# A written-out order of single instructions, first keys loaded through GpSimd, and three crossed batches instead of four

## The chip, the cores and the metric

The kernel runs on one core of a Trainium2 chip. The metric is the device time of one execution in microseconds, the median of the runs shown. A time of the profile is counted from the first instruction of the span.

## What is computed

A linear attention with random features is followed by a gated long convolution. There are 8 batches, 8 heads, 576 rows and a head size of 64; the model width is 512.

```
q_s, k_s = q * scale, k * scale
phi(x)   = exp(x @ omega.T - |x|^2/2 - max) / sqrt(128)      # 128 features
kv, z    = phi(k_s)^T v,  sum over rows of phi(k_s)
x        = (phi(q_s) kv) / (phi(q_s) z)                      # heads side by side: [8, 576, 512]
x1,x2,x3 = split(x @ w_proj)                                 # three times 512
conv     = irfft(rfft(x2, axis=rows) * rfft(filter, axis=rows))
out      = (x1 * conv * x3) @ w_out                          # [8, 576, 512] in float32
```

## The kernel before, in words

**Attention.** For every batch the first 512 rows are four runs of 128; the other 64 rows of two batches are taken together as the "left" work. The stages of a batch `b`, by the names that the code gives them with `nc.at(stage, b)`, are these:

- "load k", "load q", "load v" (`load_main`) bring the inputs, in float32 in DRAM, into bf16 tiles `kn`, `qn`, `vn`, by loads that GpSimd issues. "load kl", "load ql" and "load vl" (`load_left`) do so for the left rows. The weights `wproj` (three loads) and `wout` and the filter (tiles `yt` and `x13`) come on the same queue.
- "keys" turns `kn` to `kt` (eight transposes on TensorE into the PSUM bank `t`, copied by VectorE), multiplies by the features `om2` (the contraction has 64 rows, so two matmuls can lie beside each other in the array) and takes the exponential on ScalarE to `ek`. "left keys" makes `klt` and `ekl` in the same way.
- "values" finds a maximum over the features on VectorE (`h1`, `mx`), and scales `vn` to `vc` with its reciprocal.
- "turn queries" and "queries" do for `qn`, `qt` and `eqt` what "keys" does for the keys.
- "sums" multiplies `ek` and `vc` to `kv` (40 matmuls of 65 columns).
- "turn out" multiplies `eqt` and `kv`, divides on VectorE (`normalise`: `rden`, then `xb`) and turns the result to `xt`, which has the model width on the partitions.

**The turns.** The dictionary `CROSSED` has, for keys, queries and outputs, the first batch that is turned by a DMA transpose of SP ("cross keys", "cross queries", "cross out") and not by TensorE. For outputs it is 4: batches 4 to 7 are crossed. A crossed output is divided into a tile that shares the buffer of `h1`. One that isn't crossed is divided into `xb`, turned by TensorE in two groups of eight (`turn_back`) into the single buffer of `t`, and copied by ScalarE to `xt`.

**The gated convolution.** It is a transform by matmuls: "fold" and "rest" (sums of thirds of the rows, then a product with the middle third of `wproj`), "forward" (matmuls with tables `fwb`, `fwa`, `fwar`, `fwn`, `fwnr`, then complex products on VectorE, for which SP exchanges halves of a tile, `sw`, `xw`), "gates" (the outer thirds of `wproj`), "inverse" and "out". The tables are made on the chip: "residues" on VectorE and ScalarE (tiles `fi`, `fs`, `yt`, `xt`), "sines" on ScalarE, "tables" by transposes and VectorE copies. "filter" transforms the filter once. The matmuls write the three buffers of PSUM bank `h`, the attention writes the two of `a2`, which has two banks each.

**The start.** The first keys, batch 0's, don't come through GpSimd. `first_keys` has SP load them as float32 into a buffer of the tile `ek`, 512 KB at a time, and VectorE and ScalarE convert one half each. `first_constants` is called after it: it has GpSimd make the counters (`fi`, `x2`) and the identity that the transposes need.

**What sets the order.** The kernel does not issue as it is written. `Plan` records every instruction, with what it reads and writes; matmuls in a row into the same tile in the same stage count as one. `order` then finds the dependencies, gives every recorded instruction a due time from `PERIOD`, `STRETCH` and the tables `LEAD`, `SHIFT` and `LEAN` by stage, batch and engine, and `simulate` runs the recorded list through costs of engines, buffers and DMA queues, and at each step takes the instruction that is due first among those that can start soon. `STAY` favours 64-row matmuls while TensorE is in that form. `issue` emits the list, so every engine gets its instructions in that order and waits for each in turn. Tiles of a pool take their buffers in that order too.

All recorded instructions carry one source line in the profile, the line of `record`'s call in `issue`; they are told apart by tiles.

Of the kernel before, what the change touches and what calls it, by code (L numbers as in the profile page):

```python
# [23 lines left out]
CROSSED = {"keys": 5, "queries": 5, "out": 4}  # L24
PERIOD, STRETCH, STAY = 136.732, 16.038, 101.39
LEAD = {
    "cross keys": 0.92, "cross out": 7.64, "cross queries": -0.74, "filter": 4.65, "fold": -48.94,
    "forward": 107.85, "gates": -40.51, "inverse": 17.39, "keys": -0.75, "left keys": -52.95,
    "left out": -1.12, "left queries": -14.15, "load filter": 50.17, "load k": 55.36,
    "load kl": -1.11, "load q": -0.71, "load ql": 8.56, "load v": 0.49, "load vl": 1.73,  # L30
    "load w0": 1.61, "load w1": 5.28, "load w2": 1.64, "out": -42.88, "queries": 96.24,
    "residues": 1.41, "rest": 14.42, "sines": 0.5, "start": -189.65, "sums": -10.66,
    "tables": 0.2, "turn out": -3.18, "turn queries": 16.85, "values": -5.78, "zeros": 9.94,
}

SHIFT = {
    ("fold", 0): 48.94, ("fold", 1): 188.96, ("fold", 2): 50.05, ("fold", 7): 48.3,
    ("forward", 0): -112.16, ("forward", 1): -114.87, ("forward", 2): -107.32,
    ("forward", 6): -108.25, ("gates", 0): 16.24, ("gates", 1): 40.13, ("gates", 2): 50.94,
    ("gates", 6): 38.24, ("left keys", 2): 53.69, ("left keys", 6): 49.69, ("load k", 2): -56.64,  # L40
    ("load q", 0): -1.89, ("load ql", 0): -33.49, ("load v", 0): 2.07, ("load vl", 2): -6.7,
    ("queries", 1): -97.56, ("queries", 2): -131.03, ("queries", 6): -98.12,
    ("queries", 7): -93.75, ("rest", 1): 207.08, ("rest", 7): -14.42, ("turn out", 1): -12.03,
    ("turn out", 2): -153.32, ("turn queries", 1): -15.77, ("turn queries", 2): -16.64,
    ("values", 1): 546.29, ("values", 2): -24.51,
}
LEAN = {
    ("forward", "DVE"): 35.53, ("forward", "PE"): -40.96, ("gates", "DVE"): -10.03,
    ("gates", "PE"): 146.99, ("keys", "ACT"): -14.86, ("left queries", "ACT"): -47.8,
    ("queries", "ACT"): 5.49, ("queries", "PE"): 33.51, ("rest", "ACT"): -8.58,  # L50
    ("rest", "DVE"): -16.93,
}
# [33 lines left out]
class Op:  # L86
    __slots__ = (
        "eng", "calls", "reads", "writes", "due", "n", "busy", "lat", "deps", "users",
        "tiles", "start", "end", "name", "dma", "table", "where", "rows", "base",
    )  # L90

    def __init__(self, eng, due, n, name, where):
        self.eng, self.due, self.n, self.name, self.where = eng, due, n, name, where
        self.calls, self.reads, self.writes = [], [], []
        self.busy = self.lat = 0.0
        self.deps, self.users = {}, []
        self.tiles = set()
        self.dma = self.table = None
        self.rows = 128
# [13 lines left out]
class Plan:  # L113
# [4 lines left out]
    HOP = {"PE": 55.0, "DVE": 37.0, "ACT": 37.0, "POOL": 60.0, "SP": 60.0}  # L118

    def __init__(self, nc, tc):  # L120
        self.nc, self.tc = nc, tc
        self.ops, self.tile_of, self.slots = [], {}, {}
        self.where = "start", 0
        self.tensor = Proxy(self, "PE", nc.tensor)
        self.vector = Proxy(self, "DVE", nc.vector)
        self.scalar = Proxy(self, "ACT", nc.scalar)
        self.gpsimd = Proxy(self, "POOL", nc.gpsimd)
        self.sync = Proxy(self, "SP", nc.sync)
        self.allow_low_precision = nc.allow_low_precision
# [4 lines left out]
    def _new(self, eng, name):  # L134
        stage, b = self.where
        more = LEAD.get(stage, 0.0) + SHIFT.get((stage, b), 0.0) + LEAN.get((stage, eng), 0.0)
        op = Op(eng, more, len(self.ops), name, self.where)
        self.ops.append(op)
        return op

    def tile(self, pool, shape, dtype, name, bufs=1):
        t = pool.tile(shape, dtype, name=name, bufs=bufs)
        key = t.name if hasattr(t, "name") else t[:].tensor.name
        self.slots[pool.name, name] = bufs
        line = self.where[0]
        self.tile_of[key] = ((pool.name, name), "residues" if line == "load filter" else line)
        return t
# [7 lines left out]
    def record(self, eng, real, name, args, kw):  # L155
# [16 lines left out]
        if join:  # L172
            op = last
        else:
            op = self._new(eng, f"{name} {outs[0].tensor.name}")
            op.rows = ins[0].ap[0][1] if eng == "PE" else 128
# [5 lines left out]
        self._cost(op, eng, name, outs, ins)  # L182
        if name == "activation":
            op.table = {AF.Exp: "exp", AF.Sin: "sin"}.get(kw["func"])
        return op

    def opaque(self, eng, call, out, busy):
# [3 lines left out]
        op.busy = op.lat = busy  # L191

    @staticmethod
    def _free(ap):
        n = 1
        for _, c in ap.ap[1:]:
            n *= c
        return n

    def _cost(self, op, eng, name, outs, ins):  # L200
        out = outs[0]
        n = self._free(out)
        if name == "dma_start_transpose":
            op.busy, op.lat = 2000.0, 2200.0
            op.dma = ("HW", self._free(out) * 128 * 2 / 240.0)
            return
        if name == "dma_start":
            a = out if out.space != bass.MemoryType.DRAM else ins[0]
            run = a.ap[-1][1] * SIZE[a.dtype]
            rows = a.ap[0][1] * self._free(a) // a.ap[-1][1]  # L210
            if eng == "POOL":
                op.busy, op.lat = (880.0 if rows > 600 else 720.0), 3300.0
                op.dma = ("SW", rows * max(run, 166) / 198.0)
            elif out.space != bass.MemoryType.DRAM and ins[0].space == bass.MemoryType.DRAM:
                op.busy, op.lat = 580.0, 2300.0
                op.dma = ("HL", rows * run / 330.0)
            else:
                op.busy, op.lat = 580.0, 2000.0
                op.dma = ("HW", rows * run / 180.0 / (1 if out.space == bass.MemoryType.DRAM else 4))
            return  # L220
        half = all(SIZE[a.dtype] == 2 for a in (out, *ins))
        sbuf = all(a.space != bass.MemoryType.PSUM for a in (out, *ins))
        if eng == "PE":
            m = n / (4.8 if ins[0].ap[0][1] == 64 else 2.4) + 2.5
            op.lat = op.busy + n / 2.4 + 166.0
            op.busy += m
            return
        if eng == "DVE":
            if name == "memset":
                busy = n * SIZE[out.dtype] / 4.8 + 5.0  # L230
            elif name == "reciprocal":
                busy = 5.8 * n + 78.0
            elif name == "tensor_tensor":
                busy = n / (1.92 if half and sbuf else 0.96) + 68.0
            elif name == "scalar_tensor_tensor":
                busy = n / 0.96 + 130.0
            elif name in ("tensor_copy", "tensor_scalar", "tensor_scalar_mul"):
                rate = (4 if sbuf else 2) if half else (2 if sbuf else 1)
                if name != "tensor_copy" and not sbuf:
                    rate = 1  # L240
                busy = n / (0.96 * rate) + (68.0 if half else 100.0)
            elif name == "reduce_max":
                busy = self._free(ins[0]) / 0.96 + 60.0
            else:
                busy = n / 0.96 + 68.0
            op.busy, op.lat = busy, busy + 82.0
        elif eng == "ACT":
            busy = n * 0.8333 + (52.0 if not sbuf else 190.0)
            op.busy, op.lat = busy, busy + 107.0
        else:  # L250
            op.busy = op.lat = n / 1.2 + 100.0

    def order(self):
        last = {}
        for op in self.ops:
# [6 lines left out]
            for key, kind in ((op.reads, 0), (op.writes, 1)):  # L262
                for t, r in key:
                    last[t].append((op, kind, r))
                    if t in self.tile_of:
                        op.tiles.add(t)
        for op in self.ops:
            for o in op.deps.values():
                o.users.append(op)
        for op in reversed(self.ops):  # L270
            lat = op.lat + (op.dma[1] if op.dma else 0.0) + 50.0
            last = min((u.base for u in op.users), default=op.where[1] * PERIOD)
            op.base = last - STRETCH * lat / 1000.0
        for op in self.ops:
            op.due += op.base
            if op.eng == "PE":
# [5 lines left out]
    def simulate(self):  # L282
# [19 lines left out]
        for op in ops:  # L302
            if not op.deps:
                ready[op.eng].append(op)
# [1246 lines left out]
```

## Time and profile before

| what | us |
|---|---|
| three runs | 266.75, 267.43, 267.69 |
| median | 267.43 |
| the profiled execution | 266.88 |
| its span, first to last instruction | 264.8 |
| TensorE busy (PE) | 239.7, 91% |
| VectorE busy (DVE) | 213.4, 81% |
| ScalarE busy (ACT) | 195.2, 74% |
| GpSimd busy (POOL) | 61.3, 23% |

The granted TensorE clock is full throughout. The span is shorter than the execution's own time by 2.1 us, which lie around it. PE is TensorE's matmuls and PEld its weight loads, which overlap them. Matmuls are pipelined and their ends are modelled, so a busy PE need not be at its peak. A line of a timeline has the start, the duration, the engine, the operation, the tiles (out<-in), the shape and a count, and in brackets the idle time before it with what ended it.

### The profile page before, as it was taken

To read this page: it belongs to the slowest core of one execution; us is meant where nothing else is said; L and a number is where in the kernel's file an instruction comes from. 1 tells how busy PE (TensorE), PEld (TensorE's weight loads), DVE (VectorE), ACT (ScalarE), POOL (GpSimd) and SP (SyncE) were. 2 spreads that over 40 slices of the span, in tenths; PEclk is the share of its full clock that TensorE was granted. 3 is DMA by queue.
4 is the path that set the end of the run, shared out by engine and by line. 5 is a ranking of instruction groups with operands and counts; after the bars stand their busy time and mean duration, and the time that the engine had idled before them with its cause. 6 is when DMAs were issued, how large, how long until landed. Compare 5 with 4: busy or idle time off the path is not lost. (4 is left out here: it accounts for less than half of the span.)

```text
span 264.8 us, 5724 instructions
## 1 busy us (share of the span) xinstructions
PE 239.7 (91%) x2202; PEld 135.3 (51%) x2234; DVE 213.4 (81%) x475; ACT 195.2 (74%) x307; POOL 61.3 (23%) x86
## 2 busy tenths in 40 slices
PE   0576689999999999989999999999999999999994
PEld 0444445565476547546456454447455554446541
DVE  7999975689959999998499995979989788188470
ACT  6699499759999988986938976997495565753523
POOL 8634474444831610650040000000000000000000
PEclk9999999999999999999999999999999999999999
DMA  7999999999997978899679169524316311430406
GB/s 178 195 198 189 202 204 200 204 168 188 185 156 132 110 114 159 87 157 189 195 92 177 44 141 220 119 108 135 74 35 182 90 42 38 149 71 2 157 1 198
DMA packets 88866, 36.31 MB, mean 137 GB/s; under 512 B 60299, under 2 KB 83336, under 8 KB 88840
## 3 DMA queue, kind: packets, MB, share of 16 engines
q0 software_dynamic: 58560, 16.78, 61.4%
q1 hardware_dynamic: 30136, 19.04, 29.6%
q8 instruction: 17, 0.28, 0.4%
q10 hardware_dynamic: 144, 0.13, 0.1%
q14 instruction: 9, 0.07, 0.1%
HBM read 34.64 MB, written 9.44 MB: 166 GB/s over the span
## 5 line engine op out<-in xcount | busy, mean ns | idle before, releaser
L405 ACT CAST x<-h 128x512 bf16<-128x512 f32 x68 | 39.8, 596 | 31.5 <-PE h L405 28.4
L405 PE MATMUL h<-xt,wproj 128*128 128x512 bf16 x240 | 59.4, 380 | 1.3 <-DVE bt L405 0.4
L405 PEld LDWEIGHTS <-wproj 128*128 128x128 bf16 x384 | 31.2, 98 | 27.6 <-issue 2.7
L405 ACT ACTIVATE eqt<-a 128x1024 bf16<-128x1024 f32 x32 | 32.2, 1065 | 4.6 <-PE a L405 4.6
L405 ACT ACTIVATE osb<-h 128x512 f32<-128x512 f32 (+4 forms) x49 | 28.2, 575 | 7.3 <-PE h L405 5.9
L405 ACT ACTIVATE ek<-a 128x1024 bf16<-128x1024 f32 x32 | 32.1, 1046 | 0.5 <-PE a L405 0.2
L405 PE MATMUL h<-wproj,xf 128*128 128x512 bf16 x120 | 30.5, 379 | 1.7 <-DVE x13l L405 0.7
L405 PE MATMUL h<-wout,yt 128*128 128x512 bf16 x127 | 30.9, 379 | 0.4 <-DVE yt L405 0.3
L405 POOL DMA_DIRECT2D qn<-in_q_dram x26 | 22.9, 893 | 33.5 <-DMA qt<-qn 19.0
L405 DVE TENSOR_TENSOR x<-h,x 128x512 bf16<-128x512 f32 x32 | 21.8, 684 | 6.4 <-PE h L405 5.6
L405 DVE TENSOR_TENSOR bt<-h,osb 128x384 f16<-128x384 f32 x32 | 16.5, 552 | 7.8 <-PE h L405 5.3
L405 PEld LDWEIGHTS <-yt 128*128 128x128 bf16 x128 | 11.9, 98 | 14.8 <-issue 0.9
L405 PEld LDWEIGHTS <-xf 128*128 128x128 bf16 x134 | 12.2, 98 | 13.9 <-issue 1.5
L405 PE MATMUL h<-x,fwb 128*128 128x512 bf16 x68 | 18.3, 379 | 0.4
L405 PE MATMUL h<-gtab,xs 128*128 128x384 bf16 x64 | 15.6, 326 | 0.0
L405 PE MATMUL a<-om,kt 64*128 64x128 bf16 x256 | 11.5, 218 | 2.9 <-DVE kt L405 1.4
L405 PEld LDWEIGHTS <-eqt 128*128 128x128 bf16 x256 | 10.9, 98 | 5.7 <-DVE xb L405 1.3
L405 DVE TENSOR_TENSOR xb<-a,rden 128x512 bf16<-128x512 f32 x20 | 13.3, 684 | 0.4
L405 PE MATMUL a<-kv,eqt 128*128 128x65 bf16 x256 | 12.0, 194 | 1.0 <-DVE xb L405 1.0
L405 PE MATMUL a<-qt,om 64*128 64x512 bf16 x64 | 11.4, 383 | 0.9 <-ACT eqt L405 0.3
L405 PEld LDWEIGHTS <-kt 64*128 64x128 bf16 x256 | 7.5, 94 | 8.8 <-issue 5.5
L405 DVE TENSOR_TENSOR xf<-xt 128x1024 bf16<-128x1024 bf16 (+1 forms) x16 | 8.6, 551 | 4.2 <-ACT xt L405 4.2
(159 smaller groups left out, 471.2 us busy)
## 6 DMA issues: line engine op xcount, KB each, us to landing
out_dram<-osb SPq DMA_DIRECT2D x24, 256.0 KB, 2.3
vn<-in_v_dram POOLq DMA_DIRECT2D x8, 512.0 KB, 9.6
kn<-in_k_dram POOLq DMA_DIRECT2D x7, 512.0 KB, 8.4
qn<-in_q_dram POOLq DMA_DIRECT2D x24, 128.0 KB, 7.4
sw<-sp SPq DMA_DIRECT2D x16, 128.0 KB, 2.3
wproj<-in_moe_w_proj_dram POOLq DMA_DIRECT2D x3, 512.0 KB, 10.1
ek<-in_k_dram SPq DMA_DIRECT2D x2, 512.0 KB
qn<-in_q_dram POOLq DMA_DIRECT2D x2, 512.0 KB, 10.1
```

Source lines behind the costliest of these rows:

```text
L405: getattr(real, name)(*args, **kw)
```

## The change

It has three parts.

1. `CROSSED["out"]` is 5 in place of 4: batch 4's output is turned by TensorE and ScalarE and not by SP's DMA transpose.
2. `first_keys` is gone. Batch 0's keys are loaded by GpSimd in two halves, and converted on the way; the constants are made by a call between the two halves (the recorded position; the list below decides on the order of issue).
3. `simulate`, the costs and the tables of due times are gone. `ORDER` is a list of the numbers of all 1349 recorded instructions in the order in which they are issued, and `order` returns it.

```diff
-CROSSED = {"keys": 5, "queries": 5, "out": 4}
-PERIOD, STRETCH, STAY = 136.732, 16.038, 101.39
-LEAD = {
...
+CROSSED = {"keys": 5, "queries": 5, "out": 5}
+
+ORDER = """
+    0 28 138 55 1 29 30 136 32 2 33 26 35 4 137 27 3 5 37 31 56 11 38 39 10 22 44 7 48 45 8 49 46
+    50 6 40 52 15 23 51 34 24 84 13 139 41 42 20 47 70 43 21 71 36 77 69 85 25 9 53 86 54 73 57 72
...
+    1316 1267 1306 1265 1318 1266 1268 1269 1331 1270 1317 1332 1335 1334 1333 1338 1336 1337 1341
+    1339 1340 1344 1342 1343 1345 1346 1348 1347
+"""
...
-        return self.simulate()
...
+        order = [self.ops[int(n)] for n in ORDER.split()]
+        place = {op.n: i for i, op in enumerate(order)}
+        assert len(place) == len(order) == len(self.ops)
+        for op in order:
+            assert all(place[n] < place[op.n] for n in op.deps), "an instruction before its data"
+        return order
...
-    def first_keys():
-        nc.at("load k", 0)
-        k32 = nc.tile(att, [P, H, NT, D], FP32, name="ek", bufs=2)
-        t_ = nc.tile(nat, [P, H, NT, D], BF16, name="kn", bufs=2)
-        for g in range(2):
-            hs = slice(4 * g, 4 * g + 4)
-            nc.sync.dma_start(
-                out=k32[:, hs].rearrange("p h t d -> p h (t d)"),
-                in_=k[0, hs, 0:SM, :].rearrange("h (p t) d -> p h (t d)", t=NT),
-            )
-        for g in range(2):
-            hs = slice(4 * g, 4 * g + 4)
-            if g == 0:
-                nc.vector.tensor_copy(out=t_[:, hs], in_=k32[:, hs])
-            else:
-                nc.scalar.copy(out=t_[:, hs], in_=k32[:, hs])
-        nat_tiles["k", 0] = t_
-
-    first_keys()
-    first_constants()
+    load_main(0, "k", 2, first_constants)
     load_main(0, "q")
     load_main(0, "v")
     load_left(0, "k")
```

On each engine the two orders are alike in the large: the stages follow each other in much the same sequence. In the small nearly every engine's list differs. GpSimd's loads are the most mixed. After, they begin: half of batch 0's keys, counters, both left keys, the other half, batch 0's queries, the identity, batch 1's keys, one left value, two left queries, a piece of the filter, batch 0's values. Batch 1's values (`vn`) are the sixth load before and the twenty-fifth after.

## The prediction

> **What bounds the kernel now.** First the busy shares of the page, then its 40 slices (6.6 us each), then the busy time by stretches. In the stretches the columns are busy microseconds and instruction counts of PE, PEld, DVE, ACT and POOL.
>
> ```profile
> PE 239.7 (91%) x2202; PEld 135.3 (51%) x2234; DVE 213.4 (81%) x475; ACT 195.2 (74%) x307; POOL 61.3 (23%) x86
> ...
> PE   0576689999999999989999999999999999999994
> ...
> DVE  7999975689959999998499995979989788188470
> ACT  6699499759999988986938976997495565753523
> ```
>
> ```profile
> 10.00:15.00 5.00, 4.80 (x61) 3.94 (x61) 4.67 (x15) 3.80 (x5) 1.67 (x3) 1.00 1.45 198
> 15.00:20.00 5.00, 3.32 (x44) 1.99 (x41) 4.78 (x15) 5.00 (x7) 1.63 (x2) 1.00 1.46 198
> 30.00:35.00 5.00, 2.99 (x32) 1.60 (x34) 4.90 (x12) 2.99 (x4) 3.86 (x6) 1.00 1.34 199
> 35.00:40.00 5.00, 4.76 (x72) 3.30 (x73) 2.91 (x5) 4.68 (x8) 3.10 (x4) 1.00 1.27 205
> 140.00:150.00 10.00, 9.60 (x90) 5.53 (x90) 9.34 (x21) 8.71 (x15) 0.00 (x0) 1.00 1.03 136
> ```
>
> The kernel has two regimes. Up to about 38 us VectorE sets the pace: from 5 to 35 us it is busy 28.8 of 30 us while TensorE idles 11.7. From 40 us on TensorE sets it: all its stretches from 40 to 260 us sum to 215.45 busy of 220, so it idles 4.55 us there. The rest to 264.8 us is the tail after the last matmul (260.86): one half eviction and a store, in both kernels the same instructions. The clock is granted in full. So the time is: the moment TensorE is filled, plus its work, plus those few idle microseconds.
>
> Two prices are read from TensorE's timeline (start us, us, what; the starts are the clock, since the ends are modelled).
>
> ```profile
> 98.37 1.02 PE L405 MATMUL h<-xt,wproj 128*128 128x512 bf16 x4
> 99.23 0.61 PE L405 MATMUL t<-ident,qn 128*128 128x128 bf16 x8
> 99.68 1.03 PE L405 MATMUL h<-xt,wproj 128*128 128x512 bf16 x3
> ...
> 160.07 1.03 PE L405 MATMUL h<-wout,yt 128*128 128x512 bf16 x4
> 160.94 2.75 PE L405 MATMUL h<-xt,wproj 128*128 128x512 bf16 x12
> 163.62 0.61 PE L405 MATMUL a<-qt,om 64*128 64x512 bf16 x4
> 164.16 1.04 PE L405 MATMUL h<-xt,wproj 128*128 128x512 bf16 x4
> 165.03 1.03 PE L405 MATMUL h<-wout,yt 128*128 128x512 bf16 x4
> ```
>
> A group of eight transposes takes 99.68 - 99.23 = **0.45 us**. Four full matmuls take 0.87 us (160.07 to 160.94), 0.216 each. Twelve, followed by a 64-row block, take 163.62 - 160.94 = 2.68, 0.09 over 12 x 0.216. The block, two pairs side by side, takes 0.54, 0.11 over 2 x 0.216. So going into 64-row work and back costs **0.20 us**.
>
> **What the Trainium skill says.** (1) TensorE: Matmul & The Clock Gate, "Wait — 56ns, not 53.3ns?": warm matmuls start 55.6 ns apart for 128 columns and 215.7 for 512. The trace agrees: 0.45 / 8 = 56 ns and 216 ns. (2) TensorEngine Tiling (Array Packing), "Key Properties": changing the tiling mode drains TensorE; the 0.20 us above fits. (3) DMA: Bandwidth & Descriptors, "SWDGE vs HWDGE vs iDMA": only a GpSimd load casts, and "Issuing engines are not separate DMA queues": all issuers share 16 DMA engines. The trace agrees: behind the 1 MB of SP's uncast keys the first small kl load took 5.45 us to land.
>
> **The change part by part.**
>
> *Batch 4's outputs.* One SP transpose (kernel line "cross out") goes; two groups of eight transposes and two ACT copies come. TensorE: 2 x 0.45 = **+0.90**, on the path, since TensorE idles under 5% there. ACT: 2 x 1.02 (COPY xt<-t, 1022 ns in the groups) = 2.04, beside TensorE: ACT idles 4.6 us from 130 to 140 us. If that cover is gone, they delay the single t bank, up to 1.0 each. DVE: the same four products, into xb instead of h1 (684 and 672 ns): 0. SP: one issue of 1.8 us less; its stores come earlier, nobody waits for them: 0. New are two places where TensorE needs DVE's xb and then, in one PSUM bank, ACT's copy. In the profile such meetings cost 0.2 to 0.9 us (0.69 at 116.62 for a DVE product). I take 0.4 each, **+0.8**, bounds 0 and 2.0.
>
> *64-row blocks.* In the two orders of issue, from the first gate matmul on, I count 35 such blocks before and 33 after: 2 x 0.20 = **-0.4**, bounds -0.4 and 0. Before that point there is one more (12 to 13), under VectorE's pace: 0.
>
> *The first keys.* Gone are two SP loads of 512 KB, a DVE cast of 0.63 us and an ACT cast of 1.05; added are two POOL loads of 256 KB (written), 0.9 us of issue each. ACT's cast filled time in which ACT otherwise waited (below, 2.24 us before the 11.17 row): 0. DVE's 0.63 is a real saving. POOL now issues the first load ahead of the iotas and makes the identity after five loads, at about 6.3 us instead of 1.3. The first TensorE work (4.63, then kl's at 8.07) needs it, but kl lands at about 6, so this is covered.
>
> ```profile
> 8.33 0.60 ACT L405 ACTIVATE gtab<-xt,ph 128x384 bf16<-128x384 f16 x1
> 11.17 0.46 ACT L405 ACTIVATE x<-xt,ph 128x192 bf16<-128x192 f16 x1 [2.24 <-DVE xt L405]
> 11.53 0.44 ACT L405 ACTIVATE gta<-xt,ph 128x192 bf16<-128x192 f16 x1
> 11.98 1.28 ACT L405 ACT_TABLE_LOAD   x1
> 13.28 1.02 ACT L405 ACTIVATE ekl<-a 128x1024 bf16<-128x1024 f32 x1
> ```
>
> *The early order.* These rows show the gate of the start: residues on DVE, last sines, table load, first exponential ekl. After, memsets (vcl 0.50, hqs 0.27, fwar 0.17, small ones) stand ahead of fs, so ACT starts its residues at about 5 instead of 3.78 us and spares its cast. Adding the rows up, its three gtab sines then start near 9.0 and take 1.6, the last two 0.8, the load 1.3: ekl at 12.7 to 13.3. The second half of kt, at 13.49 before, now stands behind h1<-ekl, so after ekl: about 14.5 to 15.8. VectorE waits there for what the cast saved. Five table copies (fwb, fwa, fwar, fwnr: 1.1 us) move from 17 us to behind batch 0's last xb (32.1). So xb comes at -1.7 (no wait) to 0, and vc of batch 1, at 37.95 before, at -0.6 to +0.9. Its user sums starts at 38.69, 0.7 later. I take **0**, bounds -1.7 and +0.9.
>
> *The loads.* From 10 to 58 us POOL's loads land one after another, 2.6 to 2.8 us per 512 KB (qn 10.12, vn 12.81, kn 15.48, vn 18.28, qn 20.93 us). With these steps (0.35 per small load, 0.9 per quarter of qn) the new order lands qn 0 at 10.5, vn 0 at 17, qn 1 at 21.5, wproj 1 at 30.5, vn 1 at **34.4** (18.28 before) and the last wproj at 39.4. They are needed at 14.7, 23.4, 26.3, 42.9, 36.7 and about 47. All are in time: 0. The narrowest is vn 1, with 2.3 us.
>
> *Everything else moved* keeps its size; POOL and SP are re-sorted too, and later POOL waits are behind loads with over 3 us to spare. TensorE's 4.55 us of idle time from 40 to 260 could halve (-2.3) or grow as much; I take 0.
>
> **Sum:** +0.90 + 0.8 - 0.4 = **+1.3 us**. On the profiled execution (266.88 us, its span 264.8 plus 2.1 around it) that is 268.2. The median of the three runs is 0.55 above that execution, so 267.43 + 1.3 = **268.7 us**.
>
> **The rivals.**
>
> *Faster: the order itself pays.* Single instructions, not stages, are placed. If this halves TensorE's idle time (-2.3) and the start keeps VectorE's 0.63, the sum is 0.9 - 0.4 - 2.3 - 0.6 = -2.4: **265.0 us**. For it speaks that stalls such as 0.69 us at 116.62 are waits for one DVE product; against it that only 2% is idle. It decides once idle time from 40 to 260 us is under about 3 us.
>
> *Slower still: vn 1 is late.* It moves from POOL's sixth load to its twenty-fifth. Loads 10% slower than my steps use up its 2.3 us; each further microsecond holds vc, sums of batch 1 and all behind them on DVE. With 2 us late: **270.7 us**. Against it: the DMA engines carry the same bytes less 512 KB of fp32 keys.
>
> *No difference.* The transposes fall into waits that TensorE has anyway (0.4 of idle time from 140 to 150 us), and the blocks save 0.4: +0.1 to +0.5, **267.7 us**.
>
> **How the numbers follow.** My sum 0.40, late loads 0.18, no difference 0.17, faster 0.25. About 0.3% (0.8 us) is what a measurement of this kernel tells from no change. My sum's own range, 267.7 to 270, lies mostly beyond it: slower 0.55, same 0.20, faster 0.25. The range reaches from the faster rival (265.0, taken at 265.2) to late loads with the bank's waits at their bound, 272.0.
>
> **What would show it.** TensorE: 16 transposes t<-ident,xb more (96), idle time 40 to 260 us near 5.3. ACT: xt copies six, no CAST kn. ekl near 13 us; vn 1 landing near 34; first sums of batch 1 near 38.7. I am wrong if TensorE's idle time from 40 us falls, if it is filled over 1 us earlier, or if DVE waits for a load before 60 us.

## The result, and the profile after

| | us |
|---|---|
| after, six runs | 263.25, 264.72, 265.35, 266.06, 266.14, 266.32 |
| median after | 265.71 |
| before, beside it | 266.99 |
| ratio | 0.9924, interval 0.9897 to 0.9950 |
| after, measured once more | ratio 0.9897, interval 0.9862 to 0.9932 |
| the profiled execution of after | 266.32, its span 264.5 |

The change makes the kernel 0.8 to 1.0% faster, 2.0 to 2.8 us. I had forecast 1.3 us slower. The profiled execution is the slowest of the six, and only 0.56 us below that of before (266.88), so its trace shows a bad start as well as the gain.

The page of after: busy time of the engines, then the 40 slices.

```profile
PE 243.5 (92%) x2250; PEld 138.2 (52%) x2250; DVE 211.6 (80%) x474; ACT 194.0 (73%) x308; POOL 63.0 (24%) x88
...
PE   0665969999999999999999999999999999999994
...
DVE  6896795689968999999399897599989889279480
ACT  4796579758999997987958967996495654763533
...
PEclk9998699999999999999999999999999999999999
```

The stretches of after, with the columns as before (the number behind POOL's count is the granted clock):

```profile
10.00:15.00 5.00, 4.43 (x54) 3.34 (x54) 4.06 (x11) 4.97 (x7) 2.56 (x4) 1.00 1.56 183
15.00:20.00 5.00, 3.31 (x50) 2.20 (x48) 4.82 (x11) 4.67 (x6) 3.42 (x5) 1.00 1.57 191
20.00:25.00 5.00, 2.68 (x47) 2.07 (x46) 2.82 (x6) 2.63 (x4) 2.82 (x4) 0.90 1.39 201
25.00:30.00 5.00, 4.31 (x58) 3.60 (x55) 3.59 (x8) 3.69 (x5) 3.00 (x4) 0.50 1.45 195
30.00:35.00 5.00, 3.76 (x54) 2.47 (x52) 4.55 (x11) 1.54 (x3) 2.54 (x4) 0.92 1.60 192
35.00:40.00 5.00, 3.83 (x31) 1.73 (x33) 4.92 (x17) 5.00 (x7) 2.94 (x4) 1.00 1.30 202
140.00:150.00 10.00, 10.00 (x104) 6.08 (x100) 9.17 (x21) 8.81 (x15) 3.89 (x5) 1.00 1.61 161
```

Two things are to be seen. From 40 us on TensorE is no longer idle: its stretches from 40 to 260 us sum to 219.3 of 220. In before they sum to 215.45, but this overstates the difference, since before's trace lacks 32 matmuls (more on this under "Everything else moved" below). And from 20 to 35 us something is wrong that before doesn't have: every engine but the queues is short of work, and then the granted clock falls to half. PE's fifth slice is full only because its matmuls take twice as long.

VectorE's timeline names the wait, and the chain of waits names the load:

```profile
19.76 0.68 DVE L232 TENSOR_TENSOR h<-h 128x1024 bf16<-128x1024 bf16 x1
22.59 0.42 DVE L232 TENSOR_TENSOR vcl<-vl,vcl 64x512 bf16<-64x512 bf16 x1 [2.15 <-DMA vl<-in_v_dram]
```

```profile
5.29 7.55 DMA qn<-in_q_dram
13.12 9.44 DMA vl<-in_v_dram
```

The second half of batch 0's left values was issued at 13.12 us, landed at 22.57, and VectorE, which takes its list in order, waited 2.15 us. Behind it in VectorE's list stood the keys of batch 1 (`kt`), for which TensorE waited. TensorE's timeline, a stall and then sums at half speed:

```profile
24.00 1.04 PE L232 MATMUL a<-om,kt 64*128 64x128 bf16 x16 [2.32 <-DVE kt L232]
25.73 0.61 PE L232 MATMUL a<-qt,om 64*128 64x512 bf16 x2 [0.69 <-ACT ek L232]
26.27 0.61 PE L232 MATMUL t<-ident,ql 128*128 128x128 bf16 x4
26.67 0.26 PE L232 MATMUL a<-vcl,ekl 128*128 128x65 bf16 x1
26.74 0.41 PE L232 MATMUL a<-vc,ek 128*128 128x65 bf16 x4
26.96 0.25 PE L232 MATMUL a<-vcl,ekl 128*128 128x65 bf16 x1
```

A head's five sums come every 0.29 us here (26.67 to 26.96). In the second profile of after, where the clock is full at that time, they come every 0.16:

```profile
23.04 0.62 PE L232 MATMUL a<-om,kt 64*128 64x128 bf16 x16 [1.35 <-DVE kt L232]
24.55 0.39 PE L232 MATMUL a<-qt,om 64*128 64x512 bf16 x2 [0.89 <-ACT ek L232]
24.88 0.40 PE L232 MATMUL t<-ident,ql 128*128 128x128 bf16 x4
25.46 0.19 PE L232 MATMUL a<-vcl,ekl 128*128 128x65 bf16 x1 [0.19 <-ACT ek L232]
25.49 0.29 PE L232 MATMUL a<-vc,ek 128*128 128x65 bf16 x4
25.62 0.19 PE L232 MATMUL a<-vcl,ekl 128*128 128x65 bf16 x1
```

### The profile page after: what moved, and what is told of

Same layout as the page of the kernel before. It is cut to its first block, busy times and chain, and to the rows that moved or that the text cites. A ratio compares the mean times of both kernels' runs of the same rounds, so it can differ in the third digit from the quotient of the medians.

```text
span 264.5 us, 5749 instructions
## 1 busy us (share of the span) xinstructions
PE 243.5 (92%) x2250; PEld 138.2 (52%) x2250; DVE 211.6 (80%) x474; ACT 194.0 (73%) x308; POOL 63.0 (24%) x88
## 4 chain that ended last, share of the span: by engine, by line
PE 77%; DMA 7%; DVE 6%; ACT 5%; issue 2%; POOL 1%; SPq 1%; DVEq 0%; POOLq 0%
PE h L232 60%; PE a L232 13%; PE t L232 4%; DMA vl<-in_v_dram 4%; DMA qn<-in_q_dram 3%; ACT ek L232 2%; SPq L232 1%; DVE x L232 1%; DMA xw<-xr 1%; DVE xb L232 1%; DVE kt L232 1%; ACT qt L232 1%; POOL kn L232 1%; ACT x L232 1%; DVE yt L232 1%
## 5 line engine op out<-in xcount | busy, mean ns | idle before, releaser
L232 PE MATMUL h<-xt,wproj 128*128 128x512 bf16 x256 | 62.8, 380 | 0.0
L232 ACT ACTIVATE osb<-h 128x512 f32<-128x512 f32 (+4 forms) x49 | 27.2, 571 | 10.0 <-PE h L232 7.3
L232 PE MATMUL h<-wproj,xf 128*128 128x512 bf16 x128 | 31.7, 379 | 0.0
L232 DVE TENSOR_TENSOR xb<-a,rden 128x512 bf16<-128x512 f32 x24 | 16.3, 688 | 0.5
L232 PE MATMUL a<-kv,eqt 128*128 128x65 bf16 x256 | 12.6, 195 | 0.4 <-DVE xb L232 0.2
L232 PE MATMUL a<-vc,ek 128*128 128x65 bf16 x256 | 11.9, 200 | 0.0
```

The costliest lines, as they stand in the source:

```text
L232: getattr(real, name)(*args, **kw)
```

## The experiments

Fourteen runs followed, one of them (`after_again`) of after itself. Each ratio is a kernel's time over that of the kernel before on the same chip; times in us come from it with before's median of that series (267.5 to 267.7). Most edits move single numbers in `ORDER`. "Frozen" is the order of before written out as such a list.

| kernel | median | ratio (interval) |
|---|---|---|
| vl_early | 264.12 | 0.9864 (0.9841 to 0.9887) |
| vl_late | 267.98 | 1.0023 (1.0010 to 1.0036) |
| after_again | 264.28 | 0.9897 (0.9862 to 0.9932) |
| after_fill | 264.25 | 0.9897 (0.9869 to 0.9925) |
| vl_early_fill | 264.69 | 0.9903 (0.9881 to 0.9925) |
| after_spkeys | 263.44 | 0.9860 (0.9838 to 0.9881) |
| before_poolkeys | 270.09 | 1.0097 (1.0070 to 1.0124) |
| b_early_a_late | 264.93 | 0.9902 (0.9881 to 0.9924) |
| a_early_b_late | 266.57 | 0.9968 (0.9951 to 0.9985) |
| b_x13l | 266.30 | 0.9946 (0.9924 to 0.9967) |
| before_turn4 | 268.64 | 1.0049 (1.0028 to 1.0071) |
| before_cross5 | 275.74 | 1.0300 (1.0269 to 1.0332) |
| after_cross4 | 270.53 | 1.0096 (1.0066 to 1.0127) |
| after_cross4b | 269.26 | none: runs from 263.69 to 271.38 |

### The start: one load, earlier and later

`vl_early`, from after (12 is the second `vl` load):

```diff
-    ... 84 13 139 41 ... 88 61 12 74 ...
+    ... 84 13 12 139 41 ... 88 61 74 ...
```

> The kernel after, with one GpSimd load moved: the second half of batch 0's left values (vl) is issued directly behind its first half, some 6.6 us earlier, and nothing else. T1 (the start loses time to DVE's wait for this load, and the granted clock falls after TensorE's stall there): vl lands near 16.5 us, no stall of over 1 us on TensorE from 20 to 28 us, clock 1.00 from 25 us on, 261 to 262.5 us (after: 265.7). T2 (the wait is covered, the clock falls of itself): within 0.8 us of after. T3 (the load pushes qn of batch 1 and the weights behind it by 0.4 us each and one of them is then late): slower by 0.4 to 1.

`vl_late`, from after (the load goes behind two others, batch 1's queries the large one):

```diff
-    ... 88 61 12 74 ... 78 17 68 ...
+    ... 88 61 74 ... 78 17 12 68 ...
```

> The opposite of vl_early: the kernel after with the second vl load issued one place later on GpSimd, behind batch 1's queries, and nothing else. If the wait for vl and the fall of the clock behind it are what the start of after loses: vl lands near 24.8, DVE waits 4 to 4.5 us, TensorE stalls over 4 us, the clock falls in every run (0.975 to 0.985), 267.5 to 269.5 us. If the wait is covered and the clock falls of itself: 265.7 to 266.3, as after.

`after_again` is after, unchanged.

> The kernel after, unchanged, beside vl_late on the same chip: how far its landing of vl, its clock and its time vary from run to run. If the first six runs are typical: 265.7 us, clock 0.985 to 1.00; a profile in which vl lands before 20.5 us has no wait on DVE and a full clock. If the clock has nothing to do with vl: profiles with an early vl and a low clock, or the reverse.

| | load landed | DVE waited | TensorE stalled | mean clock of the runs | ratio |
|---|---|---|---|---|---|
| vl_early | 16.27 | 0 | none over 1.1 | 0.997 (5 runs) | 0.9864 |
| after, second profile | 21.60 | 1.18 | 1.35 | 0.994 (6 runs) | 0.9897 |
| after, first profile | 22.57 | 2.15 | 2.32 | 0.990 (6 runs) | 0.9924 |
| vl_late | 25.27 | 4.01 | 4.10 | 0.985 (22 runs) | 1.0023 |

VectorE and TensorE of vl_late, each from its timeline, and the stretches of vl_late behind it:

```profile
25.29 0.42 DVE L232 TENSOR_TENSOR vcl<-vl,vcl 64x512 bf16<-64x512 bf16 x1 [4.01 <-DMA vl<-in_v_dram]
```

```profile
26.70 1.04 PE L232 MATMUL a<-om,kt 64*128 64x128 bf16 x16 [4.10 <-DVE kt L232]
```

```profile
25.00:30.00 5.00, 2.61 (x34) 2.01 (x35) 4.61 (x10) 2.33 (x3) 3.84 (x5) 0.57 1.44 196
30.00:35.00 5.00, 4.66 (x77) 3.92 (x75) 3.62 (x8) 2.80 (x5) 2.52 (x5) 0.74 1.60 190
```

One load of 64 KB, two loads later on its queue, takes the whole gain of the change away; five loads earlier, it adds 0.9 to 1.6 us to it (264.1, where I had hoped for 261 to 262.5). In vl_late none of 22 runs has a clock over 0.987. So the wait is what the start of after loses by; how much of it is the stall and how much the fall of the clock behind it, no run separates. None of the expectations had that the landing varies so much with nothing changed on the queue: in six profiles with the start of after the load landed at 20.45, 21.35, 21.49, 21.60, 21.96 and 22.57 us. Which time a run of after shows is thus in part a matter of chance.

The wait for `vl` is not the only thing behind which the clock falls. In the second profile of after the clock is full behind the short stall and half later, from 33.6 to 37.1 us. So it is in after_spkeys (below), where nobody waits for `vl` and TensorE waits for nothing longer than 0.54 us in the 3.4 us ahead of the fall. First after, then after_spkeys, each with the 3.4 us ahead of the fall and the fall:

```profile
20.59:24.00 3.41, 1.09 (x20) 0.71 (x18) 1.41 (x4) 1.69 (x2) 2.24 (x4) 1.00 1.41 197
24.00:30.83 6.83, 6.14 (x80) 4.90 (x81) 5.22 (x9) 4.36 (x6) 3.79 (x5) 0.50 1.40 198
```

```profile
30.17:33.59 3.42, 1.98 (x22) 1.18 (x22) 3.38 (x9) 1.46 (x2) 1.08 (x2) 1.00 1.78 183
33.59:37.00 3.41, 3.41 (x20) 1.74 (x18) 3.33 (x14) 3.12 (x5) 1.87 (x3) 0.50 1.30 205
```

TensorE was busy 1.09 us of such a stretch in after, 1.98 in after_spkeys and 0.29 in vl_late, and the clock fell; but in b_x13l (below) it was busy 1.94 us from 29.72 to 33.13, and the clock stayed full. The traces do not give a bound.

Nor is the gain of after a gain of the clock. Most runs of before seem to have such a fall as well: of the 27 beside vl_late, the nine with a mean clock of 0.997 or more took 266.71 to 267.07 us, the others, at 0.984 to 0.994, took 267.46 to 269.02. The three of after's twelve runs at 1.00 took 263.25 to 263.95, so some 3 us are between the two at full clock.

`after_fill` and `vl_early_fill` add work that nobody reads:

```diff
             nc.tensor.transpose(out=pb[:, g], in_=src, identity=ident[:])
+        for _ in range(24):
+            nc.tensor.transpose(out=pb[:, 7], in_=dupf[:, 2], identity=ident[:])
```

> The kernel after with work added that nobody reads: 24 more transposes of 56 ns (1.33 us at full clock) into an unused eighth of the tables' PSUM bank, issued where TensorE waits for DVE, behind the h<-ident,xf group at 21.4 us. If TensorE's stall there is what makes the granted clock fall: clock 0.994 to 1.00 in most runs (after: 0.985 to 0.987 in four of six), 263 to 264.5 us, faster than after though it does more. If the clock falls of itself: 265.7 to 266.5. If TensorE was not really idle there: 1.3 us slower, 267.

> The 24 unread transposes of after_fill, in vl_early, where TensorE's wait for vl is gone: the control for after_fill. If the filling helps only where there is a long stall to fill: no gain on vl_early (264.1), and up to 1.3 us slower where TensorE has no room for it. If filling raises the clock everywhere, stall or not: clock 1.00 in all runs and 0.3 to 0.6 faster than vl_early, 263.5.

This did not settle what it was meant to. after_fill is as fast as after_again, so 1.33 us of idle work cost nothing there. But in its profile the load landed at 20.45 us, VectorE did not wait, and nothing shows what the filling would have done to a long stall. In vl_early the filling gained nothing either; it cost about 1.0 us, the intervals just overlapping. Whether filling a stall keeps the clock up stays open; what ties the long fall of the clock to the stall is vl_late, not these two.

### The first keys

`after_spkeys` is after with before's `first_keys`; in `before_poolkeys` the frozen order of before has after's.

```diff
-    load_main(0, "k", 2, first_constants)
+    first_keys()
+    first_constants()
```

> The order of the kernel after with the first keys as before: two SP loads of float32, one cast on DVE and one on ACT; GpSimd has two loads less. If 512 KB less on GpSimd's queue bring its later loads some 2 us earlier, vl too, and that decides: no wait for vl, clock 1.00, 263 to 264.5. If the casts' 0.63 us on DVE decide: 266 to 267.

> The order of the kernel before, with the first keys loaded and converted by GpSimd in two halves (the first ahead of all, the second behind both kl loads), both casts left out; nothing else. If DVE's cast of 0.63 us lies on the path of the start, as the prediction's row has it: 266.6 to 267.2, 0.6 better than before. If the other early order takes it back: the same. If the keys now come later (the second half lands near 9.7 us): slower by up to 1.

The keys through GpSimd cost 1.0 to 1.7 us in the order of after, and 2.6 in that of before. The second is worse than any of the three cases that I had expected. The gain of 0.63 us for VectorE that I had counted is not to be seen. In after_spkeys the second vl load lands at 18.89 us and nobody waits for it; vl_early, with GpSimd's keys, is as fast (264.12 and 263.44). So the cost is what stands behind the two added loads. In before_poolkeys all loads behind them land some 5 us later (batch 1's keys at 20.91 us, 15.48 before). TensorE of before_poolkeys, from its timeline:

```profile
20.96 0.62 PE L232 MATMUL t<-ident,kn 128*128 128x128 bf16 x8 [2.08 <-DMA kn<-in_k_dram]
```

Behind this stall the clock is half for 10.2 us, from 22.72 to 32.96, and the mean clock of all six runs is 0.979 to 0.987. So a part of the 2.6 us may be the clock's; how much was not measured.

### The start and the rest, crossed over

`b_early_a_late` has before's start (its order and its keys up to the first gate matmul) and then after's order with three crossed batches; `a_early_b_late` is the counterpart. Both are lists joined at that matmul.

```diff
-    ORDER of one kernel
+    ORDER of the one up to the first matmul of "gates" 0, then what is left in the order of the other
```

> The start of the kernel before (its order and its first keys, up to the first gate matmul), then the order of the kernel after, with three crossed batches. If the gain is in the late order: TensorE's idle time from 40 to 260 us under 1.5 us, 263 to 264.5 us. If the gain came from the start (first keys through GpSimd, order before 38 us): at or above before, 267 to 269 us.

> The counterpart: the start of the kernel after (first keys through GpSimd, its order up to the first gate matmul), then the order of the kernel before, with four crossed batches. If the gain is in the late order and the start loses: TensorE idle near 4 us from 40 us on, DVE waits for vl near 20 us, 268 to 271 us. If the start is what gains: 264 to 266 us.

The first kernel is 2.6 us faster than before, with before's start. So the gain lies in the later order, as its first theory had it, though at 264.9 it is a little above the range of that theory. The second kernel is no loss, against that theory: 0.9 us faster than before, with full work on VectorE, since here the load landed at 21.35 us, just before it was needed.

### One instruction

`b_x13l` moves one product on VectorE in the frozen order of before (736 is `x13l<-h,x` of batches 0 and 1):

```diff
-    ... 818 402 836 ... 483 396 736 823 ...
+    ... 818 736 402 836 ... 483 396 823 ...
```

> The order of the kernel before with one DVE instruction moved: the product x13l<-h,x that ends TensorE's longest stall after 45 us (0.86 us at 116.6) is issued nine DVE instructions earlier, where the kernel after has it. If a stall of TensorE in its bound stretch is time one to one: 266.8, 0.86 less than before. If the next wait takes its place (vc comes 0.7 later): the same. The prediction's faster rival rests on the first.

1.4 us faster (0.9 to 2.0), no less than the stall took. TensorE of before and then of b_x13l, from the timelines:

```profile
114.26 0.81 PE L405 MATMUL h<-x,fwb 128*128 128x512 bf16 x3
114.91 1.02 PE L405 MATMUL h<-wproj,xf 128*128 128x512 bf16 x4
116.62 1.67 PE L405 MATMUL h<-wproj,xf 128*128 128x512 bf16 x7 [0.69 <-DVE x13l L405]
```

```profile
114.04 0.81 PE L232 MATMUL h<-x,fwb 128*128 128x512 bf16 x3
114.69 2.75 PE L232 MATMUL h<-wproj,xf 128*128 128x512 bf16 x12
```

In before the next four matmuls could have begun at 114.91 + 0.87 = 115.78; they begin at 116.62. In b_x13l the twelve follow each other, and a smaller wait of 0.3 us ahead of them (114.26 in before) is gone as well: 1.15 in sum. The next wait did not take its place: batch 5's `vc` came 0.7 us later and nobody waited. The list of after has this product in this place too.

### Batch 4's outputs

`before_turn4` does the third part alone, by hand, in the frozen order: SP's transpose is left out, and two groups of transposes and two ACT copies are put in.

```diff
-    SP:  cross out 4, behind the store of "out" 1
+    PE:  turn out 4, transposes behind "out" 1 and behind "inverse" 2; ACT: two copies xt<-t behind them
```

> The order of the kernel before, frozen, with the third part of the change alone: batch 4's transpose on SP is left out, its two groups of eight transposes and two ACT copies are put into TensorE's and ScalarE's lists by hand, near 132 and 135 us. By the prediction's sum: 0.90 of transposes and 0.8 of meetings on the path, 269.3. If no meeting costs anything: 268.5. If SP's transpose had held output stores for which ACT and so TensorE waited (0.6 us at 150 us): 267.9 or less.

It costs 1.3 us (0.75 to 1.9), of which 16 x 56 ns = 0.90 are the transposes; the interval holds the case with the meetings' cost and the one without. `before_cross5` does it through before's planner:

```diff
-CROSSED = {"keys": 5, "queries": 5, "out": 4}
+CROSSED = {"keys": 5, "queries": 5, "out": 5}
```

> The kernel before, its planner and its first keys, with one number changed: three crossed outputs instead of four. If turning batch 4 on TensorE is a cost, as in the prediction's sum (0.90 of transposes, 0.8 of waits): 269.4. If it is what gains, because SP's stores no longer stand behind a transpose: 265 to 267. The planner orders all that follows anew, so stalls elsewhere may come or go by 1 us.

8 us slower, which none of the cases had: the planner orders all that follows anew. The largest of TensorE's new waits stand from 160 to 180 us, 2.6 us idle, most of it (1.74) for a product on VectorE; the rest of the 8 us was not followed up. The price of the part and the price of the order it brings are two things.

`after_cross4` and `after_cross4b` go the other way, from after (414 is SP's transpose, 802 a store):

```diff
+    ... 910 410 414 802 858 ...      # after_cross4
+    ... 910 410 802 414 858 ...      # after_cross4b
```

> The order of the kernel after, with batch 4's output crossed by SP as before: 16 transposes and two ACT copies less. If the transposes lie on TensorE's path at 0.45 us per eight, as the prediction's sum has it: 0.9 us faster than after, 264.8. If they fill idle time: the same. If the crossed tile, which shares the buffer of h1, comes later than the copies did, with all else in after's order: TensorE stalls between 125 and 160 us, slower by 0.5 to 2.

> Batch 4's output crossed by SP in the order of the kernel after, as in after_cross4, but SP issues the transpose behind the output store that it follows in the kernel before, one store later. If after_cross4's loss (4.9 us over after) came of the output stores that stood behind the transpose on SP's queue: the 4.86 us stall near 150 us shrinks to under 1.5, 264.5 to 267 us, and at 264.8 the two groups of transposes are worth the prediction's 0.9. If it came of the shared buffer of h1, the stall stays and the time is near 270.

Without 0.90 us of transposes after_cross4 is 4.6 to 5.3 us slower than after, more than any of its cases had. after_cross4b gives no clear answer: five of its runs took 268.03 to 271.38 us and one 263.69, less than the median of after. Its trace, of a run of 269.89, shows only what held up that run. SP and ScalarE of after_cross4, then VectorE of after_cross4b, from the timelines:

```profile
137.47 4.32 SPq L232 DMA_TRANSPOSE xt<-h  x1
141.88 1.50 SPq L232 DMA_DIRECT2D out_dram<-osb  x2
```

```profile
149.66 0.48 ACT L232 CAST osb<-h 128x384 f16<-128x384 f32 x1 [5.47 <-DMA out_dram<-osb]
```

```profile
153.30 0.29 DVE L232 TENSOR_TENSOR xfl<-xt 128x256 bf16<-128x256 bf16 x1 [2.95 <-DMA xt<-h]
```

In the first, two output stores stood behind the transpose on SP's queue, whose issue took 4.3 us, and landed from 149.6 us on; ScalarE needed their buffer. In the second no store holds ScalarE there any more, but the transpose itself landed 14 us after its issue (7.1 in before), and VectorE needed its data. Why it is that slow there is open: GpSimd still loads at that time in this run (2.97 us busy from 140 to 150 us, 0 in before), but in before a transpose of keys took 13.8 us, too. Whether the buffer that the crossed tile shares with `h1` plays a part stays open as well.

## Why the prediction was wrong, point by point

**Batch 4's outputs, +1.7 together: nearly right.** before_turn4 has 1.3. The transposes are on the path at their full price; of the two meetings, taken at 0.8, about 0.4 shows, which is within the noise. What failed is the remark that nobody waits for SP's stores: in after's order the crossing holds them (after_cross4). And the issue that SP is spared was taken at 1.8 us; before's trace has 4.30 for this transpose.

**64-row blocks, -0.4:** the count is right (35 before and 33 after in the traces, too); their price was not measured by itself.

**First keys and early order, 0: wrong in both parts, near in sum.** The keys cost 1.0 to 1.7. The early order gives about 1.1 (after_spkeys against b_early_a_late, intervals that just touch). ekl came at 12.54 us, a little before my range of 12.7 to 13.3:

```profile
11.24 1.28 ACT L232 ACT_TABLE_LOAD   x1
12.54 1.02 ACT L232 ACTIVATE ekl<-a 128x1024 bf16<-128x1024 f32 x1
```

**The loads, 0: the step that hid a cost.** I had qn 0 at 10.5, vn 0 at 17, qn 1 at 21.5 and vn 1 at 34.4 us; they landed at 12.84, 20.11, 25.29 and 38.37. Each was 2.3 to 4 us later than my sum, because the added halves of the keys go through the queue too: in after_spkeys, without them, the same loads landed at 10.38, 17.55, 21.78 and 35.86, near my sum. And the tile that was late, `vl`, was not in my list: I had priced the large loads and not the smallest, on which VectorE's list stands.

**Everything else moved, 0: the step that failed.** I put this term at nothing, since TensorE's idle time could grow as well as shrink. before_turn4 and b_early_a_late have the same start and both turn batch 4 on TensorE; they differ in the later order alone, and the later order brings 3.9 us. My bound was 2.3, half of 4.55 us of idle time.

Two things were wrong with that number. First, the page of before counts 2202 matmuls and 2234 weight loads: 32 matmuls are missing from the records, and gaps that they leave were read as idle. before_turn4 has the same instructions up to some 128 us and all records; from 40 to 120 us it idles 1.72, before 2.74. With 0.85 from there on in b_x13l, which has all records too, some 2.6 us were real. So my rival's point, idle time under 3 us, could not decide anything: before was there already. Second, the busy column counts short waits as work, since the ends are modelled: the 0.84 us lost at 116.62 show as 0.69.

So I counted from the starts, with 0.216 us for 512 columns (the prediction's price) and 64-row matmuls at half. before_turn4 spends 222.3 us from 40 us to the start of its last matmul on 204.2 us of work, and after_spkeys 218.8 on 204.8. That is 18.2 and 14.0 us that are not work: 4.2 less, where the idle columns from 40 us on show 3.0 and 0.7, 2.3 less. Most of the 4.2 lies in four stretches: 0.8 from 40 to 60 us, 1.1 from 100 to 120 (there b_x13l's product stands), 1.0 from 140 to 160 and 0.6 from 200 to 220. Only the second was tried by itself; which instructions make the others stays open.

Windows of before_turn4, then of after_spkeys, both with all records:

```profile
100.00:120.00 20.00, 19.02 (x228) 12.07 (x227) 19.10 (x40) 17.45 (x28) 8.03 (x10) 1.00 1.14 126
...
140.00:160.00 20.00, 19.33 (x187) 10.90 (x185) 17.62 (x42) 16.81 (x27) 0.00 (x0) 1.00 0.52 85
```

```profile
100.00:120.00 20.00, 20.00 (x253) 13.01 (x252) 19.04 (x42) 17.64 (x28) 7.05 (x9) 1.00 1.21 162
...
140.00:160.00 20.00, 20.00 (x183) 10.74 (x183) 17.97 (x43) 16.34 (x26) 1.96 (x3) 1.00 0.95 126
```

**The sum.** 1.3 for batch 4, -3.9 for the later order, -1.1 for the early one, 1.0 to 1.7 for the keys: -2.7 to -2.0, and after is at -2.8 and -2.0. Each term is the difference of two neighbours in one chain of kernels from before to after, so that the sum closes is no proof of it. The rival "the order itself pays" was the case. That its 265.0 is near the measured time is in part luck: it had 2.3 for the order, where 3.9 came, and kept 0.63 for the start, where the keys cost 1.0 to 1.7. Of "late loads" the kind of cost came, but for another tile; for vn 1 VectorE waited 0.39 us in the second profile of after and not at all in the first. And "the clock is granted in full" held for the one profiled execution of before; most of its 27 runs beside vl_late have a mean clock of 0.984 to 0.994.

**What was to show it.** 96 transposes of xb and six copies of xt came:

```profile
L232 PE MATMUL t<-ident,xb 128*128 128x128 bf16 x96 | 10.0, 248 | 0.7 <-DVE kt L232 0.5
```

```profile
L232 ACT COPY xt<-t 128x1024 bf16<-128x1024 bf16 x6 | 6.1, 1021 | 2.1 <-PE t L232 2.1
```

The sums of batch 1 start at 41.33 us in the first profile and at 39.10 in the second, not at 38.7. Two of the three signs of error came: idle time fell, and VectorE waits for a load before 60 us.

Of the notes, the Trainium skill's page TensorE: Matmul & The Clock Gate, section "HAM oscillation — how this bites in real kernels", wants no idle gap over some 3.4 us if the clock is to stay. Here the half clock is as it says (0.50), but it came behind a stall of 2.32 us, and in after_spkeys behind no wait of over 0.54 us.

## What to carry to other kernels

When a list orders single instructions, find for every in-order engine the smallest transfer that it waits for, and count all that stands before it on its queue; here the place of one load of 64 KB was worth more than the whole change. Compare the counts of matmuls and weight loads before idle time is taken as a bound on what an order can gain, since missing records look idle and modelled ends look busy. Price a part (turning a batch: 1.3 us) apart from the order in which it comes: the same part cost 1.3 us put in by hand and 8.0 with a new plan, and leaving it out of an order made for it cost over 4.

## What was not expected of the hardware

- The granted clock fell to half for 6.8 us behind a stall of 2.3 us, and what follows ran at half speed: five sums in 0.29 us and not 0.16. It also fell, for 3.4 us, behind 3.4 us in which TensorE was busy 1.98 us without any long wait (after_spkeys).
- The same load in the same place of the queue landed within 20.45 to 22.57 us in six profiles, though its moment of issue varied by less than 0.9 us (12.34 to 13.18); a wait can be there in one run and not in the next.
- The issue of a DMA transpose took 1.3 to 7.4 us of SP's time in these profiles, and it landed 4.2 to 14 us after it was issued.

The fastest kernels of the study are after_spkeys and vl_early, 1.4% below before, each after with one of its own steps taken back or one load moved.
